# Combine-weight transposes and two clears moved between the first expert products, with a new instruction order, in an attention plus mixture-of-experts kernel

## The chip, the cores and the metric

The kernel runs on one core of one Trainium2 chip. The metric is device time in microseconds (us) of one execution; the value quoted is the median of several runs. The profile shows one execution in detail: TensorE (PE, with its weight loads as PEld), VectorE (DVE), ScalarE (ACT), GpSimd (POOL), and the DMA transfers, nearly all of which SyncE (SP) issues from one queue.

## The reference, cut to what matters

```python
# 1. local/global attention, B=4, H=8, 512 local + 32 global tokens, head 64 -> x [2176 tokens, 512]
# 2. x -> SoLU block
h = x @ w_in                                  # [tokens, 1024]
solu = h * softmax(h)
ln = (solu - mean) / sqrt(var + 1e-6) * g_ln
x = ln @ w_out                                # [tokens, 512]
# 3. soft mixture of 8 experts, 4 slots each (32 slots in all)
logits = x @ phi                              # [tokens, 32]
d = softmax(logits, axis=0)                   # dispatch, over tokens
slot_input = (d.T @ x).reshape(8, 4, 512)
for e in range(8):
    h = maximum(slot_input[e] @ w1[e], 0.0)   # w1[e] [512, 1024]
    slot_out[e] = h @ w2[e]                   # w2[e] [1024, 512]
c = softmax(logits, axis=1)                   # combine, over slots
out = c @ slot_out.reshape(32, 512)
```

Everything is float32; w_in and w_out arrive as float64 words and are rebuilt on the chip.

## The kernel before

The 2176 tokens are 17 tiles of 128 rows: 16 local tiles (4 batches of 4) and one tile of the 4 x 32 global tokens. A local tile goes through scores (L739), row maxima and masking on DVE (L747), exponentials on ACT (L752), transposes of the probabilities (L769, copied at L771), products with v (L784), normalisation (L791) and a transposition into x (L795). A dense tile splits x into a high and a low part (ACT L887, POOL L888) and takes 24 products with w_in (L896), the SoLU and its statistics, transposes (L960), the logits (L981, L994, L1001), an online softmax over tokens (L1004 to L1020) and the accumulation of the slot inputs (L1027, gacc L1033). Its row softmax, the combine weights, goes into `cball` (L1049 to L1053). Each of 16 half matrices of w_in and w_out is loaded whole as integer words (`wst`) and turned into float32 by ACT (L613), POOL (L614) and three DVE instructions (L603 to L605); those of w_in are then split into high and low parts (L626, L627).

The tail is serial. After the last dense tile the accumulated slot inputs are transposed (L1093) and taken through w_out (L1112) to `sT` (L1126, L1130). The first expert layer is eight steps `f1` (group g of four experts, depth d of the contraction) of 16 products each (L1142), then Relu (L1147, L1149) and transposes (L1157) into `hidT[0]` and `hidT[1]` (L1165); these two buffers hold a block-diagonal layout and are cleared to zero by POOL beforehand (L1134). The second expert layer (L1183) is made in two pieces of 256 columns. Each piece is spread over the partitions (L1193, L1197, L1198), multiplied with the transposed combine weights `ct` (L1215), copied out by ACT (L1220) or DVE (L1222) and stored (L1228; the rows of the global tile L1230). `transpose_combine` makes `ct` for four tiles at a time: ACT writes the rounded high part into `chl` (L1069), POOL the remainder (L1070), PE transposes (L1075) and ACT copies to `ct` (L1080).

In the stretch of the serial chain PE is also given idle transposes of a constant (`warm`, L879), 57 in all.

Buffers: 47 slots of 4 KB per partition in SBUF serve nearly everything, and the six thirds of the two `k` buffers join them late. The 72 loads of expert weights (`unit`, or `k` in the trace, L550) go through one SP queue, in order; each waits until its slot is free.

The order of the instructions is written by a planner inside the program: every operation has a planned duration and a priority, one number of the list `PRIORITY` in order of creation; at each moment an engine takes the ready operation with the lowest number. What it writes is fixed at build time, and on the chip every engine runs its list in order, waiting where something is late.

Of the kernel before, what the change touches and what calls it, by code (L numbers as in the profile page):

```python
# [11 lines left out]
F32R = mybir.dt.float32r  # L12
# [11 lines left out]
NTILE = NT // 128  # L24
# [342 lines left out]
def rank(names, name):  # L367
# [6 lines left out]
CAPS = dict(h=10, p1=50, E=27, W=39, eT=17, lT=18, ln=7, q=29, u=3, v=25, wst=6, xhl=28, xp=16)  # L374
KEEP = dict(E=3, W=1, eT=2, eg=13, lT=1, ln=3, mkx=24, q=3, u=2, w=4, wo=7, wst=3, xhl=4, xp=1)
# [5 lines left out]
RATE_DMA = 405.0  # L381
PIECES = [[0, 256], [256, 256]]
FULL = 3
LASTP = -2.784
EARLY, CTP = 4, 52.505
STAY = 1.81210703096
# [120 lines left out]
def kernel_body(ctx: ExitStack, tc: tile.TileContext, q, k, v, w_in, w_out, phi, gl, w1, w2, cst, out):  # L507
    nc = tc.nc
# [374 lines left out]
    def dense_tile(j):  # L883
# [29 lines left out]
        if last:  # L913
            ended.append(col[0])
            warm(WARMS[0], col[0])
# [380 lines left out]
    for _ in range(2):  # L1296
        cta.append(slot("sb", "ct", [128, 8, 128], F32R))
# [101 lines left out]
```

## Time and profile before

| | us |
|---|---|
| median of 3 runs | 298.24 (296.47 to 298.38) |
| the profiled execution, its own time | 297.78 |
| its span, first to last instruction | 296.0 |
| PE busy in it | 265.8 |
| DVE, ACT, POOL busy | 200.7, 196.9, 102.2 |

The profile's page gives each engine's busy time, a strip of 40 slices of the span with busy tenths, granted clock and DMA rate, and the chain of waits that ended last. The views of the trace used below are waits by engine and line, tables of busy time by stretch, and timelines, in which each row is a run of like instructions, with the idle time before it and what ended that in brackets. "SPq" and "ACTq" are the queues that issue DMAs.

### The profile page before, as it was taken

To read this page: it belongs to the slowest core of one execution; us is meant where nothing else is said; L and a number is where in the kernel's file an instruction comes from. 1 tells how busy PE (TensorE), PEld (TensorE's weight loads), DVE (VectorE), ACT (ScalarE), POOL (GpSimd) and SP (SyncE) were. 2 spreads that over 40 slices of the span, in tenths; PEclk is the share of its full clock that TensorE was granted. 3 is DMA by queue.
4 is the path that set the end of the run, shared out by engine and by line. 5 is a ranking of instruction groups with operands and counts; after the bars stand their busy time and mean duration, and the time that the engine had idled before them with its cause. 6 is when DMAs were issued, how large, how long until landed. Compare 5 with 4: busy or idle time off the path is not lost.

```text
span 296.0 us, 10855 instructions
## 1 busy us (share of the span) xinstructions
PE 265.8 (90%) x4350; PEld 198.7 (67%) x4350; DVE 200.7 (68%) x746; ACT 196.9 (67%) x649; POOL 102.2 (35%) x171
## 2 busy tenths in 40 slices
PE   0277889999999999999999999999999999999980
PEld 0256567767778887787878877877787674255660
DVE  0699989999674699759986888479379851020350
ACT  2398989876799789997799766637277971010330
POOL 2588956642300626141232232235132571000000
PEclk9997999999999999999999999999999999999996
DMA  7999999634972504553983758938958726999398
GB/s 234 385 405 407 404 409 397 244 121 166 340 291 69 170 3 144 193 169 86 331 260 121 222 208 250 345 119 339 374 197 286 303 72 237 388 365 357 98 326 259
DMA packets 33010, 74.69 MB, mean 252 GB/s; under 512 B 2880, under 2 KB 15296, under 8 KB 32576
## 3 DMA queue, kind: packets, MB, share of 16 engines
q1 hardware_dynamic: 32768, 73.87, 70.3%
q8 instruction: 34, 0.56, 0.8%
q10 hardware_dynamic: 192, 0.13, 0.2%
q14 instruction: 16, 0.13, 0.1%
HBM read 67.83 MB, written 4.46 MB: 244 GB/s over the span
## 4 chain that ended last, share of the span: by engine, by line
PE 71%; DMA 12%; DVE 7%; ACT 4%; issue 3%; ACTq 1%; SPq 0%; DVEq 0%
PE h L896 30%; PE p L739 5%; PE p L784 5%; DMA k<-in_w 4%; PE p L769 4%; PE p L960 4%; DMA q<-in_q 3%; PE p L1183 3%; PE p L981 3%; DMA unit<-in_w 2%; PE p L1027 2%; PE p L859 2%; PE p L848 2%; DMA wst<-in_w_in 2%; PE p L1142 2%
## 5 line engine op out<-in xcount | busy, mean ns | idle before, releaser
L896 PE MATMUL h<-w,xhl 128*128 128x512 f32 x408 | 105.9, 404 | 0.5 <-POOL xhl L888 0.5
L896 PEld LDWEIGHTS h<-w,xhl 128*128 128x128 f32 x408 | 72.9, 189 | 17.0 <-issue 1.8
L752 ACT ACTIVATE E<-E,nmx 128x128 f32<-128x128 f32 x128 | 49.6, 393 | 3.4 <-DVE nmx L747 3.4
L739 PE MATMUL p<-k,q 64*32 64x128 f32 x1024 | 20.0, 291 | 16.0 <-DMA k<-in_k 11.9
L747 DVE CUSTOM_DVE_ANT_0 E<-p,mkx 128x128 f32<-128x128 f32 x128 | 28.7, 284 | 5.8 <-PE p L739 5.8
L917 ACT ACTIVATE u<-h,st 128x512 f32<-128x512 f32 x34 | 23.2, 688 | 11.2 <-DVE st L912 11.2
L739 PEld LDWEIGHTS p<-k,q 64*32 64x32 f32 x1024 | 15.7, 112 | 19.1 <-issue 14.0
L888 POOL TENSOR_TENSOR xhl<-xp,xhl 128x512 fp32r<-128x512 f32 x16 | 20.5, 1283 | 22.2 <-ACT xhl L887 21.9
L920 DVE SCALAR_TENSOR_TENSOR u<-h,u 128x512 f32<-128x512 f32 x34 | 23.0, 683 | 4.0 <-ACT u L917 3.9
L752 ACT ACTIVATION_READ_ACCUMULATOR E<-E,nmx 128x1 f32 x128 | 24.7, 193 | 0.0
L911 DVE TENSOR_REDUCE st<-h 128x1 f32<-128x512 f32 x34 | 22.6, 683 | 0.5 <-PE h L896 0.4
L771 ACT ACTIVATE eT<-p 128x512 f32<-128x512 f32 x32 | 18.2, 593 | 4.6 <-PE p L769 4.2
L971 POOL TENSOR_TENSOR st<-st,eps 128x1 f32<-128x1 f32 x17 | 10.3, 607 | 30.6 <-DVE st L968 29.0
L966 ACT ACTIVATE u<-ln 128x1024 f32<-128x1024 f32 x17 | 18.0, 1060 | 4.2 <-DVE ln L939 4.2
L769 PE MATMUL p<-cs,E 128*128 128x128 f32 x128 | 20.2, 293 | 0.5 <-ACT E L752 0.5
L784 PE MATMUL p<-v,eT 128*32 128x64 f32 x1024 | 19.3, 225 | 1.5 <-DMA v<-in_v 0.5
L784 PEld LDWEIGHTS p<-v,eT 128*32 128x32 f32 x1024 | 16.5, 113 | 4.8 <-issue 1.5
L769 PEld LDWEIGHTS p<-cs,E 128*128 128x128 f32 x128 | 15.7, 150 | 4.3 <-ACT E L752 1.9
L924 POOL TENSOR_SCALAR st<-st 128x1 f32<-128x1 f32 x17 | 5.2, 306 | 36.2 <-ACT u L917 29.5
L965 ACT ACTIVATE lT<-p 128x512 f32<-128x512 f32 x27 | 15.6, 598 | 2.8 <-PE p L960 2.7
L960 PE MATMUL p<-cs,ln 128*128 128x128 f32 x112 | 16.0, 277 | 0.3 <-DVE ln L939 0.3
L791 DVE TENSOR_TENSOR eT<-p,r 128x256 f32<-128x256 f32 x32 | 12.6, 416 | 4.5 <-PE p L784 4.1
(141 smaller groups left out, 549.2 us busy)
## 6 DMA issues: line engine op xcount, KB each, us to landing
unit<-in_w SPq DMA_DIRECT2D x47, 512.0 KB, 5.7
v<-in_v SPq DMA_DIRECT2D x28, 512.0 KB, 6.9
k<-in_k SPq DMA_DIRECT2D x3, 1536.0 KB, 6.7
k<-in_w SPq DMA_DIRECT2D x9, 512.0 KB, 4.7
wst<-in_w_in SPq DMA_DIRECT2D x8, 512.0 KB, 8.9
wst<-in_w_out SPq DMA_DIRECT2D x8, 512.0 KB, 9.4
out<-unit SPq DMA_DIRECT2D x8, 512.0 KB, 3.8
unit<-in_w SPq DMA_DIRECT2D x13, 256.0 KB, 6.5
```

What stands on the lines that cost most here:

```text
L739: nc.tensor.matmul(out=sp[hh][32 * c : 32 * c + 32, a2 + i, :], lhsT=Q[rows, 4 * (a2 + i) + c, :], rhs=K[rows, c, s : s + 128], start=True ...
L747: nc.vector.tensor_tensor_reduce(out=E[:, hh, a, :], in0=sp[hh][:, a, :], in1=MK(mask_kind(4 * t + a)), scale=-SCALE, scalar=3.0e38, op0=A ...
L752: nc.scalar.activation(out=E[:, hh, a, :], in_=E[:, hh, a, :], func=AF.Exp, bias=nmx[:, hh, a : a + 1], scale=-1.0, accum_out=sm[:, hh, a ...
L769: nc.tensor.transpose(out=tp[:, a, :], in_=E[:, hh, a, :], identity=I())
L771: op("ACT", 478, lambda hh=hh, tp=tp: nc.scalar.activation(out=eT[hh].ap, in_=tp.ap, func=AF.Copy), (tp,), (eT[hh],))
L784: nc.tensor.matmul(out=av[32 * c : 32 * c + 32, hh, a, :], lhsT=eT[hh][:, a, 32 * c : 32 * c + 32], rhs=V[:, (g - 1) % 2, 64 * h : 64 * h ...
L888: op("Pool", 1250, lambda: nc.gpsimd.tensor_tensor(out=xl.ap, in0=X.ap, in1=xh.ap.bitcast(F32), op=ALU.subtract), (X, xh), (xl,), port=True)
L896: nc.tensor.matmul(out=hp[n].ap, lhsT=lhs[:, kt, :], rhs=rhs[kt][n].ap, start=(kt == 0 and lhs is xh and rhs is whi), stop=(kt == 3 and lh ...
L911: op("DVE", 602, lambda n=n: nc.vector.tensor_reduce(out=part(7 + n), in_=hp[n].ap, axis=AX.X, op=ALU.max, negate=True), (hp[n],), (col[7 ...
L917: op("ACT", 664, lambda n=n: nc.scalar.activation(out=u[:, n, :], in_=hp[n].ap, func=AF.Exp, bias=nm(), scale=1.0, accum_out=part(7 + n)), ...
L920: op("DVE", 613, lambda n=n: nc.vector.scalar_tensor_tensor(out=u[:, n, :], in0=hp[n].ap, scalar=1.0, in1=u[:, n, :], op0=ALU.mult, op1=AL ...
L960: nc.tensor.transpose(out=tp[:, n, :], in_=ln[:, f // 2, 128 * (f % 2) : 128 * (f % 2) + 128], identity=I())
```

## The change: what it does

Four things.

1. The transposes of the combine weights of tiles 0 to 15 (16 of L1075, with four operations each of L1069, L1070 and L1080) were created before the weight loads and could start from the end of the last dense tile's maxima. Now they are created in the tail and may start only after the third step (g=0, d=2) of the first expert layer, by a dependence on `marks[TURN]`. The two `ct` buffers are created there too. The transposes of the seventeenth tile, which were after `sT`, get the same dependence.
2. The clears of `hidT[0]` and `hidT[1]` could start with the accumulated slot inputs and with `sT`; now they start after steps (0, 0) and (0, 3) of the first expert layer, and the buffers are taken there.
3. In the planner's model each 512 KB load of expert weights is taken to last 200 ns longer.
4. All priorities are new (1546 numbers before and after), with new caps and reserves of slots by class, and a slightly larger price in the planner for changing the tile form on PE.

```diff
-EARLY, CTP = 4, 52.505
-STAY = 1.81210703096
+TURN = (0, 2)
+ZERO = ((0, 0), (0, 3))
+STAY = 2.20991703242
+UNIT_MORE = 200.0
...
-        hidT = []
+        hidT, marks = [], {}
         for g in range(2):
-            hidT.append(slot("sb", "ln", [128, 8, 128]))
-            op("Pool", 995, lambda g=g: nc.gpsimd.memset(hidT[g].ap, 0.0), (sT if g else gt,), (hidT[g],))
...
-                op("PE", 1716, f1, [sT] + [w1b[(4 * g + j, d)] for j in range(4)], hps, heat=0.91, tiled=True, count=33)
+                op("PE", 1716, f1, [sT] + [w1b[(4 * g + j, d)] for j in range(4)], [*hps, marks.setdefault((g, d), Region(sT))], heat=0.91, tiled=True, count=33)
+                if (g, d) in ZERO:
+                    n = len(hidT)
+                    hidT.append(slot("sb", "ln", [128, 8, 128]))
+                    op("Pool", 995, lambda n=n: nc.gpsimd.memset(hidT[n].ap, 0.0), (marks[(g, d)],), (hidT[n],))
...
-        transpose_combine(range(4 * EARLY, NTILE, 4), sT)
+        for _ in range(2):
+            cta.append(slot("sb", "ct", [128, 8, 128], F32R))
+        transpose_combine(range(0, NTILE, 4), marks[TURN])
...
-    for _ in range(2):
-        cta.append(slot("sb", "ct", [128, 8, 128], F32R))
-    sch.prio += CTP
-    transpose_combine(range(0, 4 * EARLY, 4), *ended)
```

Of the new numbers three places are read below; they are plain in the list, since the n-th number belongs to the n-th operation created.

The first loads, in the order of their numbers (KB; i0 to i3 and j0 to j3 are the eight halves of w_in, o2 one of w_out, q1 the queries of tile 1, k0 and k1 parts of k of the first batch, v0 to v3 of v):

| | order |
|---|---|
| before | cs 128, i1 512, q1 256, j1 512, k1 384, mk 256, q2 256, k0 448, j3 512, i0 512, v2 512, q0 256, o2 512, v1 512, i2 512, v3 512, j0 512, q3 256, v0 512, k2 704, phi 64, i3 512, q (batch 1) 512, j2 512 |
| after | cs 128, i1 512, i0 512, q1 256, mk 256, j1 512, k1 384, k0 448, o2 512, i2 512, v3 512, q0 256, j3 512, v2 512, v1 512, j0 512, k2 704, q2 256, v0 512, i3 512, q3 256, q (batch 1) 512, j2 512 |

At the end of the kernel ACT has five copies L1220 of the last piece and four DMA issues L1230 (the global tile's rows). The copy that had the largest number of these nine (268.66, the four issues 152.61 to 187.62) now has 223.56, and the issues 127.82, 223.56, 238.70 and 264.98.

The 72 loads of expert weights had numbers from 60 on before (45 of them below 230, all below 300); now the lowest is 134, and 10 are below 300.

## Rows read from the trace of the kernel before

**Rows 1.** The page: busy time of PE, and the granted clock in 40 slices
```profile
PE 265.8 (90%) x4350; PEld 198.7 (67%) x4350; DVE 200.7 (68%) x746; ACT 196.9 (67%) x649; POOL 102.2 (35%) x171
...
PEclk9997999999999999999999999999999999999996
```
**Rows 2.** Waits, PE alone: who was waited for, us in total, times, longest
```profile
PE p L739 <- DMA k<-in_k: 11.9, 1, 11.9
```
**Rows 3.** By stretch: length, busy PE, PEld, DVE, ACT, POOL, clock, DMA share, GB/s
```profile
12.00:38.00 26.00, 19.24 (x472) 14.67 (x472) 22.74 (x86) 23.63 (x80) 21.05 (x18) 0.93 1.03 405
...
60.00:230.00 170.00, 168.66 (x2929) 133.72 (x2932) 132.48 (x522) 130.52 (x447) 53.08 (x111) 1.00 0.61 208
...
236.00:244.00 8.00, 7.94 (x95) 5.97 (x97) 5.10 (x20) 6.07 (x21) 5.45 (x11) 1.00 0.23 69
...
248.00:272.00 24.00, 23.63 (x267) 9.98 (x259) 2.19 (x6) 1.47 (x3) 0.00 (x0) 1.00 1.01 356
...
284.00:294.00 10.00, 3.74 (x29) 3.17 (x27) 3.29 (x6) 3.22 (x7) 0.00 (x0) 0.83 0.99 330
```
**Rows 4.** Timeline of DVE from the start: two rebuilds begin, then the first maxima
```profile
7.54 0.69 DVE L603 TENSOR_SCALAR p<-W 128x512 int32<-128x512 int32 x1 [5.87 <-POOL W L614]
...
9.91 0.69 DVE L603 TENSOR_SCALAR p<-W 128x512 int32<-128x512 int32 x1 [0.23 <-POOL W L614]
...
13.96 0.29 DVE L747 CUSTOM_DVE_ANT_0 E<-p,mkx 128x128 f32<-128x128 f32 x1 [1.90 <-PE p L739]
```
**Rows 5.** Waits, SP's queue from 236 to 250: us in total, times, longest
```profile
SPq L550 <- PE p L1027: 6.8, 1, 6.8
SPq L550 <- PE p L1075: 5.6, 1, 5.6
```
**Rows 6.** Chain of waits from 226 to 250, by line
```profile
by line: DMA k<-in_w 27.1%; PE p L879 15.2%; PE h L896 10.5%; issue 8.7%; ACT lT L965 8.3%; PE p L1075 8.1%; PE p L1142 7.8%; PE p L1112 7.8%; PE p L960 6.1%; PE p L1027 4.2%; PE p L1126 3.9%; ACT u L917 3.7%; PE p L981 2.7%; PE p L994 2.3%
```
**Rows 7.** Timelines of DVE, ACT, POOL and PE from 239 to 244
```profile
241.40 1.09 DVE L1033 SCALAR_TENSOR_TENSOR gacc<-gacc,co,p 128x256 f32<-128x256 f32 x2 [0.46 <-PE p L1027]
...
240.30 0.42 ACT L1069 ACTIVATE chl<-cb 128x256 fp32r<-128x256 f32 x1
...
241.32 0.72 POOL L1070 TENSOR_TENSOR chl<-cb,chl 128x256 fp32r<-128x256 f32 x1
...
242.91 0.95 POOL L1134 MEMSET ln<- 128x1024 f32 x1 [0.54 <-PE p L1075]
...
242.30 0.49 PE L1075 MATMUL p<-cs,chl 128*128 128x128 f32 x3
242.62 0.38 PE L1093 MATMUL p<-cs,gacc 128*128 128x128 f32 x2
```
**Rows 8.** Timelines of PEld and PE through the expert products, with their waits
```profile
250.14 0.13 PEld L1142 LDWEIGHTS p<-unit,lps 128*32 128x32 f32 x4 [0.30 <-issue]
251.26 0.16 PEld L1142 LDWEIGHTS p<-unit,lps 128*32 128x32 f32 x8 [0.98 <-DMA unit<-in_w]
...
256.04 0.11 PEld L1142 LDWEIGHTS p<-k,lps 128*32 128x32 f32 x1 [1.20 <-DMA k<-in_w]
...
262.50 0.59 PE L1142 MATMUL p<-unit,lps 128*32 128x512 f32 x1
...
263.03 0.33 PE L1075 MATMUL p<-cs,chl 128*128 128x128 f32 x1
...
272.44 0.40 PE L1183 MATMUL p<-unit,ln 128*32 128x256 f32 x1 [0.29 <-DMA unit<-in_w]
```
**Rows 9.** Line 550 from 230 to 273, SP's queue: loads issued, durations, first and last start
```profile
L550 SPq DMA_DIRECT2D unit<-in_w x24: 327/400/1227, 230.5 to 271.7; - x24
...
L550 SPq DMA_DIRECT2D k<-in_w x6: 341/368/368, 249.5 to 267.0; - x6
```
**Rows 10.** Timeline of ACT and its queue at the end
```profile
287.50 2.98 ACTq L1230 DMA_DIRECT2D out<-unit  x4
290.54 0.60 ACT L1220 ACTIVATE unit<-p 128x512 f32<-128x512 f32 x1 [2.57 <-issue]
```

More of the change, by code (lines that the diff above doesn't have):

```diff
@@ L373 @@
 NSLOT = 47
-CAPS = dict(h=10, p1=50, E=27, W=39, eT=17, lT=18, ln=7, q=29, u=3, v=25, wst=6, xhl=28, xp=16)
-KEEP = dict(E=3, W=1, eT=2, eg=13, lT=1, ln=3, mkx=24, q=3, u=2, w=4, wo=7, wst=3, xhl=4, xp=1)
+CAPS = dict(h=10, p1=65, E=26, W=58, eT=21, lT=10, ln=15, q=41, u=22, v=43, wst=23, xhl=48, xp=14)
+KEEP = dict(p1=3, E=2, W=22, eT=2, eg=17, lT=1, ln=3, mkx=13, u=2, v=2, w=2, wo=10, wst=23, xhl=4, xp=1)
 J0 = 0
@@ L546, in ps1, with load @@
         return slot("ps", "p1", shape)
-    def load(dst, src, nbytes, view=None, chunk=4096, rate=1.0):
-        op("SP", max(nbytes / RATE_DMA if chunk == 4096 else nbytes / 410.0 * (1 + 160.0 / chunk), 430.0), lambda: nc.sync.dma_start(out=dst.ap if view is None else view(dst.ap), in_=src), (), (dst,))
+    def load(dst, src, nbytes, view=None, chunk=4096, more=0.0):
+        op("SP", max(nbytes / RATE_DMA + more if chunk == 4096 else nbytes / 410.0 * (1 + 160.0 / chunk), 430.0), lambda: nc.sync.dma_start(out=dst.ap if view is None else view(dst.ap), in_=src), (), (dst,))
     qb, qgb, kb, vb, kr = {}, {}, [], {}, {}
@@ L865, in global_tile @@
         op("DVE", 202, lambda: nc.vector.transpose(out=X[:, :, 32 * b : 32 * b + 32], in_=x.ap.rearrange("p h (d i) -> p (h d) i", d=2)), xr, (X,))
-    mprev, late, ended, held = [None], [], [], [None]
+    mprev, late, held = [None], [], [None]
     idle = []
@@ L913, in dense_tile @@
         if last:
-            ended.append(col[0])
             warm(WARMS[0], col[0])
@@ L1258, in load_tail_weights @@
                     W = unit([128, 1024])
-                    load(W, w1[e, 128 * d : 128 * d + 128, :], 128 * 4096)
+                    load(W, w1[e, 128 * d : 128 * d + 128, :], 128 * 4096, more=UNIT_MORE)
                     w1b[(e, d)] = W
@@ L1263, in load_tail_weights @@
                 W = whole_w2[(q, e)] = unit([128, 2, 512])
-                load(W, w2[e, 256 * q : 256 * q + 256, :].rearrange("(n p) d -> p n d", p=128), 128 * 4096)
+                load(W, w2[e, 256 * q : 256 * q + 256, :].rearrange("(n p) d -> p n d", p=128), 128 * 4096, more=UNIT_MORE)
         for n0, (c0, w) in enumerate(PIECES):
```

203 rows, old and new, of the table PRIORITY are left out of this document.

## The prediction

> **What bounds the kernel now.** I read the page first: PE is busy for 265.8 us of the 296.0 us span and its clock is at the upper level except in one early slice and at the very end [rows 1]. So idle PE time is the place to look for a gain, and the waits of PE and the table by stretch say where it lies [rows 2, 3]. PE does nothing until the first scores have their keys (11.9 us), and is busy for only 19.24 of the 26 us from 12 to 38, at a mean clock of 0.93 of full speed. In that stretch ACT (23.63 of 26) and DVE (22.74) are nearly full and DMA runs at 405 GB/s: the half matrices that are rebuilt on them arrive just ahead of their use. From 60 to 230 PE is busy for 168.66 of 170 us, so a new order can win at most 1.3 us of idle time there. Then comes the serial chain to `sT` (PE looks full, partly with idle transposes L879), then the expert products from 248 on with DMA full (share 1.01, 356 GB/s), and last the output stores, again with DMA full (0.99).
>
> **The change part by part.** All sums are against the profiled execution's own 297.78 us, which is 0.46 us below the median of 298.24.
>
> *Start.* By the new numbers a third half matrix of w_in (i0) comes before the keys of the first scores. DVE is idle for 5.87, 0.23 and 1.90 us before its first maxima, and one rebuild takes 9.91 - 0.23 - 7.54 = 2.14 us [rows 4]. So DVE can do three rebuilds instead of two before the maxima: -2.14 us of later work on an engine that is nearly full. Against it, adding up the loads in the two orders, the last keys needed (k0) end at 3008 KB of traffic instead of 2752: 256 KB more, +0.65 us at 405 GB/s. i3 ends at 8832 instead of 9152 KB and j2 at 10112 instead of 10176, so the last half matrices arrive no later. I take the difference, -1.5 us; the bounds are +0.65 (nothing of the DVE time survives to PE) and -2.14.
>
> *The chain loses 16 transposes.* One costs (242.62 - 242.30) / 3 = 0.11 us of PE, start to start [rows 7], 1.76 us in all, with four ACT parts of 0.42, four POOL parts of 0.72 and four ACT copies. The chain of waits puts 8.1% of 24 us, 1.94 us, on L1075 [rows 6]. But that is PE's order, not proof that someone waited: the accumulated inputs are ready at 241.40 + 1.09 = 242.49, and their transposes L1093 start at 242.62, right behind three of the moved ones, 0.13 us later [rows 7]. The moved ones ran in time that the chain spends on other engines. I take -0.3; bounds 0 and -1.94.
>
> *Slots and loads.* In that stretch the transposes hold four `chl` slots and two `ct` slots, the clears two more. SP waits 6.8 us for the accumulation and 5.6 us for the transposes to give slots back [rows 5], and DMA moves only 69 GB/s from 236 to 244 [rows 3]. Up to eight 512 KB loads (1.47 us each at 356 GB/s) can now go there. They take away the waits in the products: the weight loads of PE come in steps of 0.13 + 0.30 = 0.43 us, and twice the idle time before one is 0.98 and 1.20, so 0.68 + 0.90 = 1.58 us late, with 0.29 us once in the second layer [rows 8]: -1.9 us. They can't give more, because nothing else waits for these weights.
>
> *The products gain 16 transposes.* +1.76 us of PE, plus changes of tile form. At 262.50 the last group of the first layer starts, the next step would be at 262.93, and a transpose starts at 263.03 [rows 8]: 0.10 us each way, 0.2 a visit; the four groups need one to four visits, I take two, +0.4. The Trainium skill, TensorEngine Tiling (Array Packing), section Key Properties, says that changing the tiling mode drains TensorE, which speaks against putting full-width transposes between column-tiled products. No row here shows a visit inside the layer; by that rule a visit would be estimated, from the rows' run-outs, at 0.59 - 0.43 = 0.16 us on the way in and at 0.33 - 0.11 = 0.22 on the way out, 1.5 us for four visits, and the sum would be 1.1 us higher.
>
> The first group is ready 0.42 + 0.72 us and two hand-overs after the third step, about one step (1.72 us) later; POOL then needs 0.72 us for each further group and 0.95 us for a clear. If PE's order puts all 16 right behind the fourth step, it waits 0.42 + 4 x 0.72 + 0.95 - 1.72 = 2.5 us. Products and transposes together: 1.76 + 0.4 - 1.9 = +0.3 us; bounds -0.5 (they fill waits that remain) and +2.6 (the DMA waits stay and there are four visits).
>
> *The clears, and the seventeenth tile's transpose.* The latter already stands behind the first layer's products and stays there. The clears: 0 us, since POOL is idle from 248 to 272 [rows 3], and 0.95 us of work must be done some ten us later. Without that cover each costs 0.95.
>
> *The end.* Four DMA issues held ACT's queue for 2.98 us, and the last copy began 2.57 us late [rows 10]; the new numbers let that copy pass ahead of two or three of the issues. I take 0, since DMA is full from 284 to 294 and the stores behind it are what ends the kernel; if DMA had room it would be -2.57, which stays as the bound.
>
> *The long middle.* New order, same work: 0, with 1.3 us either way.
>
> Sum: -1.5 - 0.3 + 0.3 + 0 + 0 + 0 = -1.5, so 297.78 - 1.5 = **296.3 us**, 0.65% below the median.
>
> **The rivals.**
> (a) *The forecast*: the start gains, the tail trades waits for work. 296.3.
> (b) *The chain gets shorter too*. If PE's full queue did delay the chain, its whole 1.94 us go, and the start gives its 2.14: 297.78 - 1.94 - 2.14 + 0.3 = 294.0. For it: PE is busy for 7.94 of 8 us from 236 to 244 [rows 3], so any chain step can meet a filled queue. Against it: the 0.13 us above.
> (c) *The change does nothing*: PE's work is the same, the transposes only move, and the start is bound by data that come no earlier (j2 gains 64 KB). 298. Here belongs a fall of the clock as well: with 1.76 us less on PE the chain may look idle. In the stretch from 12 to 38 a clock of 0.93 cost 0.07 x 26 = 1.8 us [rows 3], which would just eat the gain.
> (d) *Slower: the expert weights come too late.* From 230 on 30 loads were issued, and with DMA full in the products every 512 KB load that is not in by then lengthens them by 1.47 us [rows 3, 9]. The new numbers of these loads are far larger (the lowest 134 instead of 60, 10 instead of 72 below 300), so loads of other kinds go first and slots may be spent on them. Four loads more behind 248 cost 5.9 us: 296.3 + 5.9 = 302.2. It decides from about two loads on. Against it: numbers only rank what competes for one queue, and eight slots become free in the chain.
>
> **How the numbers follow.** Chances: (a) 0.50, (b) 0.30, (c) 0.08, (d) 0.12. About 1% (3 us) is what a measurement of this kernel can tell from no change. Of (a), 0.05 falls below 295.3 and 0.44 within 1%, 0.01 above 301.2. So faster 0.35, same 0.52, slower 0.13. The range leaves out (d) and the far side of (b), where the gains of the middle and the end come on top: 292.8 to 299.8. The likeliest case alone spans 295 to 298.
>
> **What the profile after would show.** Start: three rebuilds on DVE ahead of the first maxima, the first scores about 0.6 us later than 11.9, and PE busier than 19.24 us from 12 to 38. Chain: the time from the last L896 to the first L1142 (about 19 us now) shorter by 0.3 us if I am right, by 2 if (b) is. Loads: more than 69 GB/s between 236 and 244 and no DMA named as a wait of L1142. Products: L1075 between L1142 rows, in visits of 0.2 us beyond their 0.11 each. End: L1220 no longer behind L1230 and the same length of the last stores. I would be wrong if the middle's 1.3 us of idle grew, which nothing read here excludes, or if fewer loads were in by the first product.

## The result

The changed kernel takes 294.41 us (median; 293.33 to 296.38) where the kernel before, run beside it on the same chip, takes 297.86: a ratio of 0.989, 95% interval 0.986 to 0.993, so 1.1% faster, and 3.45 us between the medians. The forecast was 296.3, within 1% of before; the time came out just beyond that 1%, nearly where rival (b) stood, 294.0, and inside the range.

The page of the changed kernel, PE's busy time and the granted clock, where [rows 1] had 265.8 us and the same single dip near the start:

```profile
PE 264.2 (90%) x4350; PEld 199.2 (68%) x4350; DVE 200.6 (69%) x746; ACT 197.0 (67%) x649; POOL 101.6 (35%) x171
...
PEclk9999799999999999999999999999999999999997
```

PE's waits, the longest one, and then all from 236 to 275 us. Against [rows 2] the first keys come 0.1 us later, and there is no DMA behind any expert product:

```profile
PE p L740 <- DMA k<-in_k: 12.0, 1, 12.0
```
```profile
PE p L1093 <- DVE gacc L1033: 0.4, 1, 0.4
PE p L1001 <- ACT L L997: 0.3, 1, 0.3
```

Busy time by stretch, columns as in [rows 3] (length, busy PE, PEld, DVE, ACT, POOL, clock, DMA share, GB/s):

```profile
12.00:38.00 26.00, 20.25 (x475) 15.24 (x475) 22.98 (x94) 22.96 (x82) 20.41 (x18) 0.93 1.03 407
60.00:230.00 170.00, 168.83 (x2945) 133.98 (x2944) 133.03 (x524) 132.62 (x448) 51.74 (x110) 1.00 0.61 207
236.00:244.00 8.00, 7.23 (x83) 4.66 (x81) 3.88 (x15) 2.59 (x12) 2.84 (x8) 1.00 0.85 282
248.00:272.00 24.00, 24.00 (x299) 12.13 (x291) 2.71 (x7) 4.26 (x10) 4.00 (x6) 1.00 0.96 318
```

PE is a whole microsecond busier from 12 to 38 at the same clock of 0.93, the middle is as it was, the loads move 282 GB/s from 236 to 244 instead of 69, and PE has no gap from 248 to 272.

One table tells where the 3.7 us between the two profiled spans lie. The marks are instructions of PE, read from its timeline; the last column is what the prediction's sum had there.

| stretch | before | after | difference | sum had |
|---|---|---|---|---|
| up to the end of the last token product (L896, after L897) | 228.43 | 228.51 | +0.08 | -1.5 (start) |
| from there to the first expert product | 19.11 | 16.54 | -2.57 | -0.3 |
| first layer | 15.56 | 13.94 | -1.62 | +0.3 |
| between the layers | 2.38 | 3.57 | +1.19 | (in the +0.3) |
| second layer to its last product | 17.57 | 16.87 | -0.70 | (in the +0.3) |
| end | 12.95 | 12.87 | -0.08 | 0 |

The marks of the two largest stretches, the last token products and the first expert product, in before and then in after (228.43 is 226.81 + 1.62, and 228.51 is 226.88 + 1.63):

```profile
226.81 1.62 PE L896 MATMUL h<-w,xhl 128*128 128x512 f32 x6
...
247.54 0.62 PE L1142 MATMUL p<-unit,lps 128*32 128x512 f32 x1
```
```profile
226.88 1.63 PE L897 MATMUL h<-w,xhl 128*128 128x512 f32 x6
...
245.05 0.62 PE L1140 MATMUL p<-unit,lps 128*32 128x512 f32 x1
```

The start went as described: three rebuilds on DVE before the first maxima (the first fence: their first instructions, and the first maximum), and the first scores on PE (the second), against [rows 2, 4]:

```profile
7.59 0.69 DVE L604 TENSOR_SCALAR p<-W 128x512 int32<-128x512 int32 x1 [5.92 <-POOL W L615]
...
9.65 0.69 DVE L604 TENSOR_SCALAR p<-W 128x512 int32<-128x512 int32 x1
...
11.71 0.69 DVE L604 TENSOR_SCALAR p<-W 128x512 int32<-128x512 int32 x1
...
14.12 0.29 DVE L748 CUSTOM_DVE_ANT_0 E<-p,mkx 128x128 f32<-128x128 f32 x1 [0.27 <-PE p L740]
```
```profile
12.03 1.96 PE L740 MATMUL p<-k,q 64*32 64x128 f32 x64 [12.03 <-DMA k<-in_k]
```

The third rebuild filled the gap of 1.90 us that [rows 4] show, for 0.16 us of delay of the first maximum in these two executions.

At the end of the chain the transposes of `gacc` no longer stand behind moved ones, as in [rows 7], but PE waits for their input:

```profile
240.18 0.44 PE L1093 MATMUL p<-cs,gacc 128*128 128x128 f32 x2 [0.42 <-DVE gacc L1033]
```

The transposes were not where the prediction put them. PE's timeline, the end of the first layer and the start of the second:

```profile
258.38 0.61 PE L1140 MATMUL p<-unit,lps 128*32 128x512 f32 x3
258.92 0.44 PE L1075 MATMUL p<-cs,chl 128*128 128x128 f32 x2
259.19 0.60 PE L1159 MATMUL p<-cs,hid 128*128 128x128 f32 x4
259.63 0.27 PE L1075 MATMUL p<-cs,chl 128*128 128x128 f32 x1
...
260.18 1.36 PE L1075 MATMUL p<-cs,chl 128*128 128x128 f32 x11
...
262.25 0.38 PE L1075 MATMUL p<-cs,chl 128*128 128x128 f32 x2
262.56 1.27 PE L1187 MATMUL p<-unit,ln 128*32 128x256 f32 x17
```

Sixteen of the seventeen transposes L1075 (2 + 1 + 11 + 2) stand behind the whole first layer, among the transposes of the activations (L1159), which have the same form; the other one follows at 271.87, in the second layer. None goes between two products of the first layer. Against [rows 8] there are no steps late for DMA.

SP's waits from 236 to 250, against the 6.8 and 5.6 us of [rows 5]: the transposes are gone from the list.

```profile
SPq L551 <- PE p L1027: 3.3, 1, 3.3
SPq L551 <- PE p L1140: 2.9, 1, 2.9
SPq L551 <- PE p L1112: 2.8, 1, 2.8
```

ACT's last rows: no copy stands behind all the issues, as one did in [rows 10], and the end is as long as before.

```profile
283.93 1.22 ACTq L1234 DMA_DIRECT2D out<-unit  x2
284.42 0.59 ACT L1224 ACTIVATE unit<-p 128x512 f32<-128x512 f32 x1
285.19 0.66 ACTq L1234 DMA_DIRECT2D out<-unit  x1
```

### The profile page after: what moved, and what is told of

Read it like the earlier page. It is cut to its first block, busy times and chain, and to the rows that moved or that the text cites. A ratio compares the mean times of both kernels' runs of the same rounds, so it can differ in the third digit from the quotient of the medians.

```text
span 292.3 us, 10850 instructions
## 1 busy us (share of the span) xinstructions
PE 264.2 (90%) x4350; PEld 199.2 (68%) x4350; DVE 200.6 (69%) x746; ACT 197.0 (67%) x649; POOL 101.6 (35%) x171
## 4 chain that ended last, share of the span: by engine, by line
PE 78%; DMA 9%; ACT 5%; DVE 4%; issue 1%; SPq 0%; POOL 0%; DVEq 0%; POOLq 0%
PE h L897 32%; DMA q<-in_q 5%; PE p L1187 5%; PE p L1140 5%; PE p L740 4%; PE p L770 4%; PE p L785 4%; PE p L960 4%; DMA wst<-in_w_in 4%; ACT E L753 3%; PE p L1027 3%; PE p L981 3%; PE p L860 2%; PE p L849 2%; PE p L1219 2%; PE p L880 1%
## 5 line engine op out<-in xcount | busy, mean ns | idle before, releaser
L897 PE MATMUL h<-w,xhl 128*128 128x512 f32 x408 | 107.0, 405 | 0.8 <-POOL xhl L889 0.6
L897 PEld LDWEIGHTS h<-w,xhl 128*128 128x128 f32 x408 | 72.7, 189 | 18.3 <-issue 2.6
L740 PE MATMUL p<-k,q 64*32 64x128 f32 x1024 | 21.4, 300 | 15.7 <-DMA k<-in_k 12.0
L748 DVE CUSTOM_DVE_ANT_0 E<-p,mkx 128x128 f32<-128x128 f32 x128 | 29.3, 284 | 7.0 <-PE p L740 6.9
L740 PEld LDWEIGHTS p<-k,q 64*32 64x32 f32 x1024 | 16.6, 115 | 20.6 <-issue 14.9
L971 POOL TENSOR_TENSOR st<-st,eps 128x1 f32<-128x1 f32 x17 | 10.9, 641 | 25.5 <-DVE st L968 25.4
L785 PE MATMUL p<-v,eT 128*32 128x64 f32 x1024 | 18.0, 222 | 0.0
L785 PEld LDWEIGHTS p<-v,eT 128*32 128x32 f32 x1024 | 15.7, 111 | 2.8 <-issue 1.2
L960 PE MATMUL p<-cs,ln 128*128 128x128 f32 x112 | 16.2, 275 | 0.0
```

Source lines behind the costliest of these rows:

```text
L740: nc.tensor.matmul(out=sp[hh][32 * c : 32 * c + 32, a2 + i, :], lhsT=Q[rows, 4 * (a2 + i) + c, :], rhs=K[rows, c, s : s + 128], start=True ...
L748: nc.vector.tensor_tensor_reduce(out=E[:, hh, a, :], in0=sp[hh][:, a, :], in1=MK(mask_kind(4 * t + a)), scale=-SCALE, scalar=3.0e38, op0=A ...
L785: nc.tensor.matmul(out=av[32 * c : 32 * c + 32, hh, a, :], lhsT=eT[hh][:, a, 32 * c : 32 * c + 32], rhs=V[:, (g - 1) % 2, 64 * h : 64 * h ...
L897: nc.tensor.matmul(out=hp[n].ap, lhsT=lhs[:, kt, :], rhs=rhs[kt][n].ap, start=(kt == 0 and lhs is xh and rhs is whi), stop=(kt == 3 and lh ...
L960: nc.tensor.transpose(out=tp[:, n, :], in_=ln[:, f // 2, 128 * (f % 2) : 128 * (f % 2) + 128], identity=I())
```

## The experiments

Executions of one kernel differ by some 3 us (after: 293.33 to 296.38), nearly all of it before the last token product, whose end lies between 227.4 and 230.7 us in the profiled executions of eight kernels that share after's order. So stretches are compared stretch by stretch, and whole times by medians and by ratios to before, run beside each kernel.

### One part alone: the transposes and clears moved, the order kept

```diff
 # after, with before's PRIORITY, CAPS, KEEP, STAY
-UNIT_MORE = 200.0
+UNIT_MORE = 0.0
+    # -265000000 as the number of each of the 16 transposes on PE
```

> The kernel before with nothing changed but the place of the 16 transposes (with their parts, behind the first expert layer) and of the two clears; the old numbers, caps and load prices stay. Theory A (the moved transposes made the gain: TensorE is never idle between the last token product and the first expert product, so each transpose there costs its whole 0.11 us, and the buffers of their parts kept expert weights from being loaded): that stretch 1.8 us shorter than the 19.1 of before, the first layer at most 14.6 instead of 15.5, the stretch between the layers 3.6 instead of 2.5, in all 1 to 2 us under before. Theory B (the gain is that of the new order alone, the transposes ran in idle time as the prediction had it): the stretch ahead of the experts 0.3 us shorter, the one between the layers 1.2 us longer, in all about 1 us over before.

Measured: 298.21 us, ratio to before 1.002 (0.999 to 1.005). From the last token product to the first expert product 19.27 us (before 19.11); first layer 13.94 and second 16.66, without waits; between the layers 4.29; end 12.95.

What follows. Both theories are half right. Leaving the chain under the old order, the 16 transposes shorten it by nothing, as the prediction had it and against theory A. Leaving it, they do take the waits out of the products: -1.62 and -0.91 us, against +1.91 between the layers. In the stretches behind the first product that makes -0.62 us, and the whole kernel isn't faster. (Its last token product ended at 230.20 us, 1.77 later than before's. Up to there PE, ACT, DVE and POOL run the same instructions in the same order in both kernels, so this is how far two executions lie apart, and not the edit.) So the part of the change that its name tells of does not bring the 3.45 us.

Where the chain's time lies, shows in the busy times from the last token product to the write of `gacc`, in before, in this kernel and in after (columns as above):

```profile
228.43:242.62 14.19, 13.59 (x161) 10.47 (x159) 10.93 (x40) 11.78 (x38) 9.08 (x21) 1.00 0.63 220
```
```profile
230.19:244.55 14.36, 12.78 (x148) 8.95 (x146) 10.62 (x40) 10.11 (x32) 6.26 (x17) 1.00 0.79 288
```
```profile
228.51:240.18 11.67, 10.98 (x138) 7.93 (x137) 9.16 (x36) 8.02 (x29) 4.46 (x13) 1.00 1.00 356
```

Without the transposes PE, ACT and POOL each have less to do (12.78 for 13.59, 10.11 for 11.78, 6.26 for 9.08), and the stretch is as long as ever. In after there are also fewer instructions of the token tiles left in it: 36 on DVE instead of 40.

### The transposes back under the new order

```diff
-        transpose_combine(range(0, NTILE, 4), marks[TURN])
+        transpose_combine(range(0, 16, 4), *ended)
+        transpose_combine(range(16, NTILE, 4), sT)
```

> The kernel after with the 16 transposes and their parts back ahead of the expert layers, with the numbers that they had before; all other numbers are those of after, and the planner orders it anew. Theory A: 1.8 us more ahead of the experts, 1 to 1.6 us more in the first layer because loads start later, 1.2 us less between the layers, in all some 2 us over after. Theory B: 0.3 us more ahead of the experts, 1.2 us less between the layers, so about 0.9 us under after. As the planner was not tuned for this mix, a longer time speaks for A only where the stretches show it.

Measured: 299.70 us, ratio 1.005 (1.002 to 1.009). The chain takes 19.04 us, the layers 14.34 and 14.02, between them 2.25, the end 19.26. This settles nothing: with six more buffers taken the planner finds another order from the last tiles to the last store, and second layer and end together, where no transpose was moved, are 3.5 us longer than in after. That the new order needs the buffers is possible; it wasn't isolated.

### The clears back

```diff
-nc.gpsimd.memset(hidT[n].ap, 0.0), (marks[(g, d)],), (hidT[n],))
+nc.gpsimd.memset(hidT[n].ap, 0.0), (sT if n else gt,), (hidT[n],))
```

> The kernel after with the two clears back at their old releasers. Both theories: the same time as after within 0.5 us, since GpSimd is idle around the first layer; the clears disturb something only if the time rises by more.

Measured: 294.62 us, ratio 0.989 (0.984 to 0.994); every stretch from the last token product on within 0.06 us of after's. The clears are worth nothing either way.

### Sixteen idle transposes more, and sixteen less

```diff
+    MORE = {1217: 1, 1219: 3, 1286: 3, 1291: 1, 1294: 1, 1296: 5, 1382: 1, 1303: 1}
+    for i, n in MORE.items():
+        def more(f=sch.ops[i].fn, n=n):
+            f()
+            for _ in range(n):
+                nc.tensor.transpose(out=idle[0].ap, in_=I(), identity=I())
+        sch.ops[i].fn = more
```

> The kernel after with 16 more idle transposes (of the identity into the PSUM buffer that nothing reads) between the last token product and the first expert product, at the places where the combine weights' transposes stood before; order, loads and buffers stay those of after. Theory A (TensorE's queue is full there): this stretch grows by 16 x 0.11 = 1.8 us from 16.5, and nothing else changes. Rival (the transposes run in idle time, the prediction's term of 0.3 us): it grows by 0.3 us.

Measured: 295.82 us, ratio 0.993 (0.990 to 0.996). The stretch is 17.35 us, 0.81 more than in after.

```diff
+    for i in [1258, 1274, 1276, 1279, 1283, 1285, 1290, 1292, 1297, 1302, 1386, 1388, 1395, 1396, 1397, 1398]:
+        sch.ops[i].fn = lambda: None
```

> The kernel after with 16 of the 44 idle transposes left out that keep TensorE busy between the last token product and the first expert product. Theory A (TensorE's full queue sets this stretch): 16 x 0.11 = 1.8 us less. Theory C (formed after the first four runs: the stretch is set by the work of the last token tiles on ScalarE and VectorE that stands behind the last token product, of which the new order leaves less): within 0.5 us of after's 16.5. A clock below 1.00 in the stretch or in the first layer would be a loss of its own.

Measured: 293.70 us, ratio 0.988 (0.981 to 0.995). The stretch is 16.17 us, 0.37 less, with the clock at 1.00. So a transpose in this stretch is worth 0.37 / 16 = 0.02 to 0.81 / 16 = 0.05 us, not the 0.11 that it takes of PE: most of it lies in time that the chain spends elsewhere. This is the quickest of the kernels that ran more than once, but its interval and after's overlap nearly whole.

### One idle transpose left

The same edit with 43 of the 44; one is left.

> The kernel after with 43 of the 44 idle transposes between the last token product and the first expert product left out. Theory C: the stretch of 16.5 us shrinks by 0.4 to 1.2 us at most, as what waits is on ScalarE and VectorE. If TensorE's clock is granted less after a stretch with gaps: granted clock below 1.00 in the first layer, which then takes up to twice its 13.9 us.

Measured: 297.80 us, ratio 0.999 (0.995 to 1.004): the whole gain is gone. The stretch is 18.72 us and the first layer 16.76. Busy times around the fall:

```profile
235.00:236.00 1.00, 0.48 (x4) 0.37 (x3) 0.55 (x4) 0.91 (x4) 0.63 (x2) 1.00 1.00 406
...
237.00:238.00 1.00, 0.75 (x13) 0.37 (x17) 0.48 (x3) 0.38 (x3) 0.66 (x3) 1.00 0.98 363
...
239.00:240.00 1.00, 0.63 (x2) 0.29 (x2) 0.31 (x1) 0.00 (x0) 0.00 (x0) 0.50 0.98 223
...
248.00:250.00 2.00, 2.00 (x16) 0.53 (x12) 0.00 (x0) 0.00 (x0) 0.00 (x0) 0.50 0.33 133
...
252.00:253.00 1.00, 1.00 (x12) 0.24 (x8) 0.00 (x0) 0.00 (x0) 0.00 (x0) 0.92 0.97 381
```

Up to the write of `gacc` nothing is lost: its transposes start 239.37 - 227.72 = 11.65 us after the last token product, as they do with 28 fills left. But with PE busy for 0.48 to 0.75 of each microsecond, the clock goes from 1.00 to 0.50, 2.4 to 1.2 GHz. It stays there until 252, through the gate products (3.64 us for the 1.93 of after) and the first 5.7 us of the first layer, and PE is busy for all of 248 to 252 before it rises. The ten executions bear this out: they range from 295.56 us at a mean clock of 0.986 to 299.64 at 0.963. The fall that rival (c) spoke of exists; the fills kept it away in after, and 28 of them did so too.

### The start undone in part: the third rebuild late again

```diff
+    for i in (12, 13, 14):
+        order.remove(i)
+    at = order.index(157) + 1
+    order[at:at] = [12, 13, 14]
```

> The kernel after with nothing changed but the third rebuild of a half-matrix (its VectorE work and the two splits that read it) put back behind the first four maxima in the order that is emitted, as it stood before; its load stays early. Theory A (the start is worth about 1 us, and what is gained there is kept up to the experts): TensorE idles 1.0 to 1.5 us more between 12 and 60 us, and the time rises by about 1 us. Rival (what the start gains is eaten up by the work of the last token tiles on ScalarE and VectorE, which set the end of that stretch): the same time as after within 0.4 us.

Measured: 296.46 us, ratio 0.997 (0.993 to 1.001), against after's 0.989: 0.0078 x 297.9 = 2.3 us lost, and with both intervals (0.0038 and 0.0036, so 0.0052 together) 0.8 to 3.9. All stretches from the last token product on are after's to 0.01 us. DVE's start in it, then PE's first token product in it, in after and in before:

```profile
11.45 0.69 DVE L604 TENSOR_SCALAR p<-W 128x512 int32<-128x512 int32 x1 [1.80 <-POOL W L615]
...
14.03 0.29 DVE L748 CUSTOM_DVE_ANT_0 E<-p,mkx 128x128 f32<-128x128 f32 x1 [0.43 <-PE p L740]
```
```profile
29.16 0.73 PE L897 MATMUL h<-w,xhl 128*128 128x512 f32 x2
```
```profile
27.72 0.73 PE L897 MATMUL h<-w,xhl 128*128 128x512 f32 x2
```
```profile
29.14 0.73 PE L896 MATMUL h<-w,xhl 128*128 128x512 f32 x2
```

DVE waits 1.80 us for its second rebuild and 0.43 before the first maximum, 2.23 in all, about as long as in before (0.23 + 1.90 = 2.13, [rows 4]); the waits lie elsewhere. The load of i0, and ACT's and POOL's parts of its rebuild, still come early, so the start isn't undone as a whole. The first token product starts 1.44 us later than in after, at the time that it had in before. PE's busy times from 12 to 60 us say nothing here: they are 39.60 us in this kernel and 41.83 in after, but the clock dips in after's execution (mean 0.96) and not in this one (1.00), and at the lower clock the same work keeps PE busy for longer (the gate products above: 3.64 us for 1.93). The loss comes out at the end of the kernel: theory A, whose 1 us lies within the interval.

### The place of the last token product

```diff
+    order.remove(1240)
+    order.insert(order.index(1170), 1240)
```

> The kernel after with one TensorE instruction group moved: the last token product goes ahead of eight transposes of the last tile but one, so that 24 transposes stand behind it as before, and not 16. Theory C, in its narrow form (what stands behind the last token product sets the stretch): the product ends 0.9 us earlier, the eight transposes and the copies that wait for them come 1.4 us later, the first expert product starts 0.5 to 2 us later, and the time rises by as much. Rival (the stretch is set by the last tile's own chain, which starts with this product): the first expert product starts 0.5 to 0.9 us earlier.

Measured: 294.51 us, ratio 0.990 (0.987 to 0.994), 0.3 us over after by the ratios, give or take 1.5. That is too coarse for the question, but the profiles decide it. PE's timeline in after, then in this kernel, from a group of products that stands ahead of the moved ones in both:

```profile
221.36 1.68 PE L897 MATMUL h<-w,xhl 128*128 128x512 f32 x6
...
225.98 1.03 PE L960 MATMUL p<-cs,ln 128*128 128x128 f32 x8
```
```profile
223.48 1.66 PE L897 MATMUL h<-w,xhl 128*128 128x512 f32 x6
...
226.61 2.98 PE L897 MATMUL h<-w,xhl 128*128 128x512 f32 x12
229.43 1.03 PE L960 MATMUL p<-cs,ln 128*128 128x128 f32 x8
...
247.93 0.62 PE L1140 MATMUL p<-unit,lps 128*32 128x512 f32 x1
```

The stretch behind the last token product grows from 16.54 to 18.34 us, 1.80 of the 2.57 by which before and after differ. But from the common group to the first expert product it is 245.05 - 221.36 = 23.69 us in after and 247.93 - 223.48 = 24.45 here, only 0.76 more; in the six other profiles of this section in which PE's order and fills from that group to the first expert product are after's, it is 23.64 to 23.69. So theory C in its narrow form is borne out (0.5 to 2 us later were expected), and its rival is not. The other 1.80 - 0.76 = 1.04 us is the mark itself, which the new order has shifted. "From the last token product to the first expert product" can't be read as it stands: of the -2.57 us, 1.04 are no gain, and about 1.5 are.

### The loads held back

```diff
+    late_loads = [1325, 1314, 1360, 1329]
+    ...                                   # emitted behind operation 1392
+    def hold(f=sch.ops[1325].fn):
+        nc.sync.dma_start(out=phb[:, 0, 0:1], in_=sch.ops[1392].outs[0].parent.ap[:, 256:257])
+        f()
```

> The kernel after with four loads of expert weights and all that follow them on SP held until the first half of the gate product's result is written (about 242.5 us in after), by a small transfer of 512 bytes that reads it, so that as many are issued ahead of the first layer as before. Order and buffers stay. Theory A (before's waits of 1.6 us in the first layer came from weights loaded late, because the parts of the transposes held the buffers): the first layer grows from 13.9 to 15.5 us or more, and the second may start later by as much as the loads then lag; 1.6 to 4 us over after. Rival (the waits came from the order of the products, not from the loads): the first layer stays at 13.9 us.

Measured: 302.86 us, ratio 1.020 (1.013 to 1.028). The first layer takes 22.74 us, 8.80 more than in after, and everything behind it is as in after. SP's wait, the traffic, PE's wait, and PE's clock behind that wait (the last but two of the columns):

```profile
SPq L1314 <- DVE ln L1116: 11.8, 1, 11.8
```
```profile
236.00:244.00 8.00, 7.23 (x87) 4.82 (x89) 5.00 (x19) 4.03 (x15) 2.79 (x9) 1.00 0.27 108
```
```profile
PE p L1140 <- DMA unit<-in_w: 4.8, 1, 4.8
```
```profile
254.00:260.00 6.00, 5.11 (x24) 1.19 (x28) 0.00 (x0) 1.29 (x4) 1.28 (x3) 0.50 1.04 406
```

The mechanism is theory A's: the first layer is fed by the loads that are issued in the chain. Its price was far too low, for two reasons. The hold, 11.8 us, was longer than before's waits. And the 8.80 us are not all waiting: PE stands still for 4.8 us, and when its products go on, from 254.89, the clock is at 0.50 until about 260.8, which over those 5.9 us costs some 3 (an estimate: half of them). The profiled execution is the slowest of the four (305.48 at a mean clock of 0.975; the fastest, 302.08, had 0.990). Late loads, rival (d)'s cause, do cost time; they just didn't happen in the change.

### The price of a change of form

Sixteen idle transposes inside the first layer, four visits of four, then one of sixteen:

```diff
+    MORE = {1408: 4, 1409: 4, 1419: 4, 1420: 4}     # then: {1409: 16}
```

> The kernel after with 16 idle transposes in the first expert layer, four each behind four of its eight steps: four visits from products in 128x32 form to transposes of 128x128 and back, nothing else changed. By the prediction's price (0.11 a transpose, 0.2 a visit for the two form changes) the layer grows by 1.76 + 0.8 = 2.6 us. [...] With nothing for the change of form: 1.8 us.

> The kernel after with 16 idle transposes in the first expert layer as one visit behind its third step of the first group (four visits of four gave 2.91 us). With 0.11 a transpose and a price of 0.3 for each visit: the layer grows by 1.76 + 0.3 = 2.0 us. If the change of form costs nothing and a transpose costs more there: 2.9 us again.

Measured: 16.85 and 15.98 us for the layer of 13.94, so +2.91 and +2.04; each kernel 296.86 us. PE's timeline at one visit of the first, then of the second kernel:

```profile
249.95 0.66 PE L1312 MATMUL p<-cs 128*128 128x128 f32 x4
```
```profile
255.91 1.97 PE L1312 MATMUL p<-cs 128*128 128x128 f32 x16
```

With the same 16 transposes the three further visits cost 2.91 - 2.04 = 0.87, so 0.29 us a visit, and (2.04 - 0.29) / 16 = 0.109 us a transpose. The prediction had 0.2 for a visit, the estimate from run-outs 0.38; the truth is in the middle. TensorEngine Tiling (Array Packing) of the Trainium skill, section Key Properties, says that a change of tiling mode needs a drain; these runs agree that it isn't free.

### The last copy behind the issues

Only the number of ACT's last copy is changed, to one above those of its four issues.

> The kernel after with the last of ScalarE's copies of the output behind the four transfers that ScalarE issues, as it stood before. The prediction's value: the end behind the last product stays at 12.9 us, as the DMA engines are full there; its bound: up to 2.6 us more.

Measured, in one run: 293.48 us, the end 12.87 us as in after. ACT's timeline in it:

```profile
283.03 1.91 ACTq L1230 DMA_DIRECT2D out<-unit  x3
284.98 0.60 ACT L1220 ACTIVATE unit<-p 128x512 f32<-128x512 f32 x1 [1.36 <-issue]
```

The copy waits 1.36 us for the issues, as [rows 10] showed with 2.57, and nobody behind it notices. The value 0 was right, and the bound of 2.57 can be dropped.

## Why the prediction was right, and where it was not

The sign, the range and the list of places were right; the time was 1.9 us off because two terms were mis-sized, the products and the chain. Step by step:

*Start, -1.5: the mechanism right, the size not far off.* Put back, the third rebuild costs 2.3 us (0.8 to 3.9), an interval that holds 1.5. The profiles tell the two parts of the term apart. The first scores come at 11.95 to 12.56 us in the twelve profiles with after's loads and at 11.16 and 11.88 in the two with before's (before, and the transposes moved alone): 0.7 later on the mean, where the sum took 0.65. (Before and after alone would show 0.15, too little because single executions differ by more than that.) From the first scores to the first token product it is 15.1 to 15.9 us in the eleven profiles with the early rebuild and 17.2 to 17.3 in the three without it: 1.7 less on the mean, where the sum took 2.14. Together that is -1.0. In the first line of the table (+0.08) it is hidden: when the last token product ends, PE has already done eight transposes L960 that before still has to do (16 left instead of 24), and by the swap the mark stands 1.04 us later for this.

*The chain, -0.3: right for the transposes, and for the stretch a step that failed.* Taken out under the old order, the transposes give nothing (19.27 for 19.11); as fills they are worth 0.02 to 0.05 us each under the new one. But without the moved mark the stretch is 2.57 - 1.04 = 1.53 us shorter. The prediction counted only the transposes here and put the new order of the other work at nothing ("New order, same work: 0"). By the swap, 0.76 us of it comes from the new place of the last token product. The other 0.77 is what 18.34 us, with the product at its old place, lies below before's 19.11; which of the reordered steps or missing transposes brings it, no run isolates. Rival (b) had 1.94 us here, but for the full queue of PE, and sixteen transposes more cost 0.81, not 1.94. That its 294.0 is near the measured time is luck: it had 2.14 us at the start and +0.3 in the products.

*Slots and loads, -1.9: right.* No product waits for DMA any more, and the loads run at 282 GB/s where it was 69. The two layers got 1.62 + 0.70 = 2.3 us shorter. The move alone already brings that (13.94 and 16.66 us), and holding the loads takes it away with interest.

*The products gain 16 transposes, +1.76 + 0.4: the other step that failed.* They were taken to stand between products, with visits of their own. They stand between the layers, among transposes of the same form, so there is no further change of form; and four idle transposes that stood there before are gone: sixteen L1075 stand there where one did, so (15 - 4) x 0.109 = 1.2 us, measured 1.19. Had they been inside the layer, a visit would have cost 0.29, more than the 0.2 taken. With the waits removed, the term is -1.62 + 1.19 - 0.70 = -1.1 where the sum had +0.3.

*Clears 0, end 0, middle 0: right.* The first two were tested; of the middle, PE's 168.83 busy of 170 us against 168.66 is all there is. (The order of the last token tiles, which that term also left at 0, counts under the chain.)

With the sizes of the profiles, -1.0 for the start, -1.5 for the chain and -1.1 for the products make -3.6 us, beside -3.45 between the medians. The last two rest on stretches that repeat within 0.1 us in the kernels that share after's order; the share of the start in the whole time is only known as 0.8 to 3.9 us.

*The rivals.* (c) needed the clock to fall; it did where all fills but one were taken out, and not in after. (d) needed late loads; DMA was early instead.

## What to carry to other kernels

When a diff moves some work and renumbers all the rest, price the first few microseconds of the new order as carefully as the moved work: here one rebuild that fills a gap of 1.9 us before the first maxima was worth 0.8 to 3.9 us, while moving the 16 transposes alone won nothing that could be measured (298.21 us for 297.72). Of moved work, price what it holds as well as what it runs: here its buffers delayed the weight loads, while its engine time was nearly free. And compare stretches between marks that the change cannot shift; a stretch from "the last product" says little if the products were reordered, but one from an earlier product that kept its place showed 0.76 us where whole times could not.

## What the runs showed that was not expected

The new dependence of the clears and parts on `marks` orders only the planner: it writes no data that an instruction would wait for. POOL's timeline of after has the first clear at 243.19, behind the gate products, and the first expert product starts at 245.05.

```profile
243.19 0.95 POOL L1146 MEMSET ln<- 128x1024 f32 x1 [4.13 <-PE p L1112]
```

The idle transposes are no decoration: with 28 of 44 the clock stayed at 1.00 and the time at 293.7 us; with one of 44 it was 0.50 for some 13 us and cost all that the change had won.
